# Gated scan and two feed-forward layers in one kernel: weight conversions of item 0 two steps sooner, the second chunk's tokens turned on TensorE

## The chip, the cores and the metric

The kernel runs on one core of a Trainium2 chip. The metric is the time of one execution on the device in microseconds (us), from the first instruction to the last result in memory; the median of several runs is quoted. A core has five engines that run their own instruction streams in order and wait for each other on semaphores: TensorE (PE in the profile, with its weight loads as PEld), VectorE (DVE), ScalarE (ACT), GpSimd (POOL) and SyncE (SP), which here issues most of the DMAs.

## The reference

Three stages follow one another over 2 x 6080 tokens of width 256:

```python
sig = 1.0 / (1.0 + np.exp(-f_logit))
f = lower_bound + (1.0 - lower_bound) * sig
h = f[:, t] * h + (1 - f[:, t]) * x[:, t]      # for each t in turn; y[:, t] = h
h1 = y @ w_in1;  z = (h1 - np.tanh(h1)) @ w_out1      # 256 -> 2048 -> 256
h2 = z @ w_in2;  out = np.maximum(0.01 * h2, h2) @ w_out2
```

Tokens, gates and output are fp32. The four weight matrices arrive as 64-bit floats and have to be turned into pairs of short fp32 numbers (a high and a low part) on the chip.

## The kernel before

**Chunks and items.** The 12160 tokens are cut into chunks of 1024. An *item* is one chunk in one of the two feed-forward layers; items 0 and 1 are chunks 0 and 1 in layer 0, item 2 is chunk 0 in layer 1, and from then on layer 0 of the next chunk and layer 1 of the one before alternate. Each item has 8 *units* (256 columns of the hidden width). Every product is done with high and low parts, as three fp32r matmuls.

**Steps of the first three items.** Items 0, 1 and 2 are plain products, written as four *steps* a unit, 32 steps an item, numbered s = 0 to 95. A step computes one 128 x 512 block of the hidden layer. In program order, step s issues: `plain(s)`, twelve LDWEIGHTS and MATMULs shown as six pairs or "x2" rows (line L441), into a PSUM bank from the list `hb`; on ScalarE the tanh `act(s)` (L451); on VectorE `shrink(s)` (L459, h - tanh h), which is the last reader of the bank; then for the step before, `hi(s-1)` on ScalarE (L464) and `lo(s-1)` on VectorE (L469); then the side jobs of that step, `work(s)`; and last, for the step three back, `emit_B(s-3)` (L485), which multiplies its hidden block by the unit's output weights `wb` into the banks `acc`. So TensorE sees plain(s), B(s-3), plain(s+1), B(s-2) and so on, and B(s-3) needs lo(s-3) and the unit's `wb`.

**Side jobs.** `put(p, jobs, q)` spreads a list of jobs evenly over the steps p to q - 1. During item 0 there are two sorts. *Conversions*: `first[u + 1]` turns the raw words of the input weights of unit u + 1 (`wa`) and the output weights of unit u (`wb`) into high and low parts. It has a load of 1 MB and eight jobs: s0 (ScalarE, L116), s1 (VectorE, L120 and L121), s2 (L127), s3 (L132, and two casts on ScalarE, L135), s4 (L138), s5 (L143) and twice s6 (L149), which write the low parts of `wa` and of `wb` and issue their copies to DRAM. In item 0 `wb` of unit u is read for the first time by B(4u), issued in step 4u + 3. *The front of chunk 1*: tokens of f_logit and x are loaded in pieces of 32 x 32 x 32 elements (`load_tokens`), turned on VectorE (L338), passed through tanh (L345), an affine gate with the columns `ga` and `gb` (VectorE, L349), a product (L356), and the scan (L367); then they are split into high and low parts (L396, L400).

**Start.** Chunk 0 is loaded in rows of 256 elements by `first_front` in two halves of 512 tokens; TensorE turns 128 x 128 blocks against an identity (L296) into PSUM banks that are not yet in use, and tanh, gate, product and scan (L302, L306, L310, L320) follow. Four loads are issued from ScalarE's DMA queue, three from SyncE's, all at the beginning.

Of the kernel before, what the change touches and what calls it, by code (L numbers as in the profile page):

```python
# [15 lines left out]
P = 128  # L16
# [4 lines left out]
def tile_gated_scan_two_ffn(  # L21
# [77 lines left out]
    def convert(parts):  # L99

        s = {}
        n = 2 * len(parts)
        sh = [P, 4, 2 * P]

        def words(i, dt):
            return s["raw"].bitcast(dt).rearrange("p a (n t) -> p a n t", t=2)[:, :n, :, i]

        def f0():
            s["raw"] = cv.tile(sh, U64, tag="raw", bufs=2, name="raw")
            for i, (src, _, _) in enumerate(parts):  # L110
                nc.sync.dma_start(s["raw"][:, 2 * i:2 * i + 2], src)

        def s0():
            s["t"] = cv.tile(sh, F32, tag="c", bufs=2, name="b")
            s["b"] = s["t"][:, :n]
            nc.scalar.activation(s["b"], words(1, F32), AF.Abs)  # L116

        def s1():
            b = s["b"].bitcast(I32)
            nc.vector.tensor_scalar(s["b"], s["b"], W_LO, W_HI, op0=ALU.max, op1=ALU.min)  # L120
            nc.vector.tensor_scalar(  # L121
                b, b, 3, 0x3FFFF000, op0=ALU.logical_shift_left, op1=ALU.bitwise_and
            )
# [12 lines left out]

        def s4():
            nc.vector.scalar_tensor_tensor(  # L138
                words(0, F32), words(0, U32), 2.0**-32, words(1, I32), op0=ALU.mult, op1=ALU.add
            )  # L140

        def s5():
            nc.vector.tensor_scalar(  # L143
                words(1, I32), s["b"].bitcast(I32), -(1 << 23), None, op0=ALU.bitwise_and
            )

        def s6(i):
            l, e = (words(j, F32)[:, 2 * i:2 * i + 2] for j in range(2))
            nc.vector.scalar_tensor_tensor(  # L149
                s["w"][i][1], l, 2.0**-20, e, op0=ALU.mult, op1=ALU.mult  # L150
            )
            parts[i][2]()

        return f0, [s0, s1, s2, s3, s4, s5] + [lambda i=i: s6(i) for i in range(len(parts))]
# [123 lines left out]
                src[t0:t0 + n, d0:d0 + 32].rearrange("(i c) r -> c i r", c=32),  # L278
            )

    def first_front(half, banks):

        t0, a = macros[0][0], half * H
        nb = H // P
        s = {}

# [3 lines left out]
                s[nm], {"f": ff, "x": xf}[nm][t0 + a:t0 + a + H].rearrange("(j p) d -> p j d", p=P)  # L290
            )

        def turn(nm):
            for k in range(KD):
                for j in range(nb):
                    nc.tensor.transpose(  # L296
                        banks[nm][k][:, j * P:(j + 1) * P], s[nm][:, j, k * P:(k + 1) * P], ident
                    )

        def s1(k):  # L300
            s["g", k] = fp.tile([P, H], F32, tag="f", bufs=2, name="g")
# [1 line left out]

        def s2(k):
            g = s["g", k]
            nc.vector.tensor_scalar(g, g, ga[:, k:k + 1], gb[:, k:k + 1], op0=ALU.mult, op1=ALU.add)  # L306

        def s4(k):
            s["v", k] = fp.tile([P, H], F32, tag="x", bufs=2, name="v")
# [2 lines left out]
            )  # L312

        def s5(k):
            if 0 not in ys:
                ys[0] = fp.tile([P, KD, 2 * H], F32, tag="y", name="y")
            y = ys[0][:, k]
            for p in range(0, H, H // 2):
                m = p + H // 2
                nc.vector.tensor_tensor_scan(  # L320
                    y[:, a + p:a + m], s["g", k][:, p:m], s["v", k][:, p:m],
                    y[:, a + p - 1:a + p] if a + p else 0.0, op0=ALU.mult, op1=ALU.subtract,
                )
            if half:
                nc.vector.tensor_copy(carry[:, k:k + 1], y[:, 2 * H - 1:2 * H])

        return load, turn, [lambda f=f, k=k: f(k) for f in (s1, s2, s4, s5) for k in range(KD)]

    def front(c, k):

# [214 lines left out]
    with tc.manual_schedule():  # L545
# [46 lines left out]
        put(4 * I + 16, [lambda: conv.__exit__(None, None, None)])  # L592


        for it in range(len(items) - 1):
            base = I * it
            l, c = items[it + 1]
            jobs = []
            if l == 0:
                at = ((8, 14) if it == 0 else (base - 4, base + 2))  # L600
# [3 lines left out]
            lead = 10 if it == 0 else 0 if l == 0 else 2 * NS  # L604
# [150 lines left out]
```

## Time and profile before

| | |
|---|---|
| median of 3 runs | 2047.53 us (2045.61 to 2047.65) |
| profiled execution | 2048.42 us, its span (first to last instruction) 2046.6 us |
| TensorE busy in the span | 1990.6 us, 97% |
| VectorE, ScalarE busy | 1429.3 us (70%), 1199.8 us (59%) |
| mean granted TensorE clock | 0.987 of full speed |
| chain that ended last | 91% TensorE, 5% VectorE |

The profiled execution is 0.9 us above the median, and 1.8 us of it lie outside the span. Shares of busy time over the whole span hide where TensorE waits; the stretches of the span have to be read one by one. A granted clock of 1.00 is 2.4 GHz, and the lower of the two levels is 1.2 GHz.

### The profile page before, as it was taken

To read this page: it belongs to the slowest core of one execution; us is meant where nothing else is said; L and a number is where in the kernel's file an instruction comes from. 1 tells how busy PE (TensorE), PEld (TensorE's weight loads), DVE (VectorE), ACT (ScalarE), POOL (GpSimd) and SP (SyncE) were. 2 spreads that over 40 slices of the span, in tenths; PEclk is the share of its full clock that TensorE was granted. 3 is DMA by queue.
4 is the path that set the end of the run, shared out by engine and by line. 5 is a ranking of instruction groups with operands and counts; after the bars stand their busy time and mean duration, and the time that the engine had idled before them with its cause. 6 is when DMAs were issued, how large, how long until landed. Compare 5 with 4: busy or idle time off the path is not lost.

```text
span 2046.6 us, 24457 instructions
## 1 busy us (share of the span) xinstructions
PE 1990.6 (97%) x8744; PEld 1652.0 (81%) x8744; DVE 1429.3 (70%) x2269; ACT 1199.8 (59%) x2185; POOL 0.7 (0%) x6
## 2 busy tenths in 40 slices
PE   5879999999999999999999999999999999999998
PEld 4668888888888888888888888888888888889887
DVE  6788887986776776776677677577677677666443
ACT  3445655665666566566566556566656656656554
POOL 0000000000000000000000000000000000000000
PEclk8989999999999999999999999999999999999999
DMA  4536777784563563563554555456356356354352
GB/s 158 150 134 216 233 240 257 267 260 133 173 180 142 162 183 142 162 183 141 163 170 155 162 162 162 142 169 175 142 162 183 141 162 178 142 162 170 141 162 86
DMA packets 384458, 348.30 MB, mean 170 GB/s; under 512 B 289104, under 2 KB 291152, under 8 KB 384336
## 3 DMA queue, kind: packets, MB, share of 16 engines
q1 hardware_dynamic: 382480, 345.17, 52.5%
q10 hardware_dynamic: 1856, 1.57, 0.2%
q8 instruction: 69, 1.13, 0.2%
q14 instruction: 53, 0.43, 0.1%
HBM read 309.07 MB, written 37.62 MB: 169 GB/s over the span
## 4 chain that ended last, share of the span: by engine, by line
PE 91%; DVE 5%; DMA 1%; ACT 1%; issue 1%; SPq 1%; DVEq 0%; ACTq 0%
PE acc L485 48%; PE b L428 22%; PE c L428 16%; PE b L441 3%; PE c L441 2%; DVE gl L469 1%; DVE g L459 1%; DVE raw L138 0%; SPq L508 0%; DMA out_dram<-o 0%; ACT b L116 0%; DMA wb<-st 0%; DVE b L127 0%; DMA wb<-wb 0%; ACT gh L464 0%
## 5 line engine op out<-in xcount | busy, mean ns | idle before, releaser
L485 PE MATMUL acc<-gh,wb 128*128 128x512 f32 (+1 forms) x3072 | 1043.9, 389 | 26.4 <-DVE wb L149 24.5
L485 PEld LDWEIGHTS acc<-gh,wb 128*128 128x128 f32 x3072 | 579.2, 189 | 146.0 <-DVE wb L149 27.3
L469 DVE TENSOR_TENSOR gl<-g,gh 128x512 fp32r<-128x512 f32 (+1 forms) x768 | 500.5, 679 | 222.5 <-ACT gh L464 214.3
L485 PE MATMUL acc<-gl,wb 128*128 128x512 f32 (+1 forms) x1536 | 597.2, 389 | 1.8 <-DVE gl L469 1.8
L464 ACT CAST gh<-g 128x512 fp32r<-128x512 f32 (+1 forms) x768 | 444.8, 615 | 86.7 <-DVE g L459 86.6
L428 PE MATMUL b<-xh,wa 128*128 128x512 f32 (+1 forms) x1344 | 492.6, 387 | 0.0
L428 PE MATMUL c<-xh,wa 128*128 128x512 f32 (+1 forms) x1008 | 362.6, 387 | 0.0
L485 PEld LDWEIGHTS acc<-gl,wb 128*128 128x128 f32 x1536 | 289.8, 189 | 61.2 <-DVE gl L469 3.8
L453 ACT ACTIVATE g<-c 128x512 f32<-128x512 f32 (+1 forms) x280 | 159.6, 602 | 247.2 <-PE c L428 226.1
L428 PEld LDWEIGHTS b<-xh,wa 128*128 128x128 f32 x1344 | 252.3, 188 | 49.2
L451 ACT ACTIVATE g<-c 128x512 f32<-128x512 f32 (+1 forms) x272 | 155.4, 602 | 209.8 <-PE c L428 168.2
L428 PE MATMUL b<-xl,wa 128*128 128x512 f32 (+1 forms) x672 | 260.0, 387 | 0.0
L428 PEld LDWEIGHTS c<-xh,wa 128*128 128x128 f32 x1008 | 189.2, 188 | 37.0
L459 DVE TENSOR_TENSOR g<-c,g 128x512 f32<-128x512 f32 (+1 forms) x272 | 177.7, 678 | 38.2 <-ACT g L451 35.3
L715 DVE TENSOR_TENSOR c<-b,s 128x512 f32<-128x512 f32 (+1 forms) x168 | 115.1, 685 | 116.2 <-PE b L428 114.5
L428 PE MATMUL c<-xl,wa 128*128 128x512 f32 (+1 forms) x504 | 195.0, 387 | 0.0
L661 ACT COPY c<-b 128x512 f32<-128x512 f32 (+1 forms) x168 | 94.9, 565 | 131.0 <-PE b L428 131.0
L695 DVE TENSOR_TENSOR c<-b,s 128x512 f32<-128x512 f32 (+1 forms) x168 | 116.1, 691 | 56.3 <-PE b L428 32.9
L459 DVE TENSOR_TENSOR g<-b,g 128x512 f32<-128x512 f32 (+1 forms) x112 | 76.4, 682 | 111.7 <-ACT g L451 111.5
L428 PEld LDWEIGHTS b<-xl,wa 128*128 128x128 f32 x672 | 126.1, 188 | 24.9
L684 ACT COPY s<-c 128x512 f32<-128x512 f32 (+1 forms) x168 | 98.1, 584 | 37.7 <-PE c L428 30.2
L428 PEld LDWEIGHTS c<-xl,wa 128*128 128x128 f32 x504 | 94.6, 188 | 18.6
(76 smaller groups left out, 1182.5 us busy)
## 6 DMA issues: line engine op xcount, KB each, us to landing
wa<-wa SPq DMA_DIRECT2D x168, 896.0 KB, 5.0
wb<-wb SPq DMA_DIRECT2D x192, 512.0 KB, 5.6
wa<-wa SPq DMA_DIRECT2D x24, 512.0 KB, 5.5
wa<-st SPq DMA_DIRECT2D x24, 512.0 KB, 3.4
out_dram<-o SPq DMA_DIRECT2D x176, 64.0 KB, 1.9
rawf<-in_f_logit_dram SPq DMA_DIRECT2D x80, 128.0 KB, 5.7
rawx<-in_x_dram SPq DMA_DIRECT2D x80, 128.0 KB, 3.0
raw<-in_moe_w_in_dram SPq DMA_DIRECT2D x16, 512.0 KB, 6.0
```

Of the source, the lines that this page charges most:

```text
L428: nc.tensor.matmul(bank[:, :h], wt[:, s, w], xx[:, v, :h], start=start and i == 0, stop=i == 2, skip_group_check=True,)
L441: nc.tensor.matmul(bank[:, :h], wt[:, s, 2 * k + j], xx[:, v[k], :h], start=i == 0, stop=i == 5,)
L451: nc.scalar.activation(g[:, :h], src[:, :h], AF.Tanh)
L453: nc.scalar.activation(g[:, :h], src[:, :h], AF.Prelu, alpha=0.01)
L459: nc.vector.tensor_tensor(g[:, :h], u["src", name][:, :h], g[:, :h], ALU.subtract)
L464: nc.scalar.copy(gh[:, :h], u["g", name][:, :h])
L469: nc.vector.tensor_tensor(gl[:, :h], u["g", name][:, :h], u["hi", name][:, :h].bitcast(F32), ALU.subtract)
L485: nc.tensor.matmul(bank[e][:, :h], w[:, j, s, es], v[:, :h], start=first and i == 0, stop=i == 2, skip_group_check=True,)
L661: nc.scalar.copy(c11[:, :h], b1[:, :h])
L684: nc.scalar.copy(s5[:, :h], c12[:, :h])
L695: nc.vector.tensor_tensor(c12[:, :h], b1[:, :h], s5[:, :h], ALU.add)
L715: nc.vector.tensor_tensor(c22[:, :h], b1[:, :h], s5[:, :h], ALU.add)
```

## The change

Five things change in the program. (1) In item 0 the conversion that writes `wa` of unit u + 1 and `wb` of unit u (u from 2) is put into steps 4u - 2 to 4u instead of 4u to 4u + 2, and its load at step 4u - 7 instead of 4u - 5; that of u = 1 into steps 2 to 4 instead of 3 to 5. (2) Chunk 1 is no longer loaded in small pieces and turned on VectorE: `first_front` gets the chunk as an argument, loads rows of 256 elements from SyncE's queue, and TensorE turns them, four 128 x 128 blocks at a time, into the bank `c12`, each of eight groups as a side job of a step between 9 and 28. `c12` leaves the list `hb`, which has three banks instead of four for all of items 0, 1 and 2. (3) The affine gate of both chunks becomes an ACTIVATE with Identity on ScalarE, with `ga` and `gb` as columns. (4) The first loads are reordered: SyncE issues the first raw weights and then x; ScalarE issues f_logit, `lower_bound`, and, behind its first three activations, the second raw weights and the second half of chunk 0. (5) Item 1 begins like item 0 with the order `order0`: four steps on the first half of the chunk over two units, then four on the second half.

```diff
-        def f0():
+        def f0(eng=nc.sync):
...
-                nc.sync.dma_start(s["raw"][:, 2 * i:2 * i + 2], src)
+                eng.dma_start(s["raw"][:, 2 * i:2 * i + 2], src)
...
-    def first_front(half, banks):
+    def first_front(c, half, banks):
...
-        t0, a = macros[0][0], half * H
+        t0, a = macros[c][0], half * H
...
-        def turn(nm):
-            for k in range(KD):
-                for j in range(nb):
...
+        def turn(nm, k):
+            for j in range(nb):
+                nc.tensor.transpose(
+                    banks[nm][k][:, j * P:(j + 1) * P], s[nm][:, j, k * P:(k + 1) * P], ident
+                )
...
-            nc.vector.tensor_scalar(g, g, ga[:, k:k + 1], gb[:, k:k + 1], op0=ALU.mult, op1=ALU.add)
+            nc.scalar.activation(g, g, AF.Identity, scale=ga[:, k:k + 1], bias=gb[:, k:k + 1])
...
-        load0("f", nc.sync)
-        load0("x", nc.scalar)
-        first[0][0]()
-        load1("f", nc.scalar)
-        first[1][0]()
-        load1("x", nc.scalar)
...
+        first[0][0]()
+        load0("f", nc.scalar)
+        load0("x", nc.sync)
         nc.scalar.dma_start(lb, lower_bound.rearrange("(k p) -> p k", p=P))
...
-        run(front0[0:2] + first[0][1][0:2] + front0[2:4] + first[0][1][2:4] + front0[4:8])
-        run(mix(split0[0:4], first[0][1][4:]))
+        run(first[0][1][0:1])
+        for nm in "fx":
+            turn0(nm, 0), turn0(nm, 1)
+        for k in range(KD):
+            front0[k][0]()
+        first[1][0](nc.scalar)
+        for nm in "fx":
+            load1(nm, nc.scalar)
+            turn1(nm, 0), turn1(nm, 1)
+        for k in range(KD):
+            front0[k][1]()
+        run(first[0][1][1:5])
+        run([front0[k][i] for i in (2, 3) for k in range(KD)])
+        run(mix(split0[0:4], first[0][1][5:]))
...
-        put(1, front1 + split0[4:8], 4)
-        put(3, first[2][1], 6)
+        put(1, mix(*front1) + split0[4:8], 4)
+        put(2, first[2][1], 5)
         for u in range(2, NU):
-            put(NS * u - 5, [first[u + 1][0]])
-            put(NS * u, first[u + 1][1], NS * u + 3)
-
+            put(NS * u - 7, [first[u + 1][0]])
+            put(NS * u - 2, first[u + 1][1], NS * u + 1)
+
+        split1 = make_forms(1)
         I = NS * NU
+        for half, a in ((0, 9), (1, 21)):
+            load, turn, stages = first_front(1, half, {nm: [c12, c12] for nm in "fx"})
+            put(a - 4, [lambda load=load, nm=nm: load(nm, nc.sync) for nm in "fx"], a - 3)
+            jobs = []
+            for k in range(KD):
+                f = stages[k]
+                jobs += [
+                    lambda turn=turn, k=k: turn("f", k), f[0], lambda f=f: (f[1](), None),
+                    lambda turn=turn, k=k: turn("x", k), f[2], f[3],
+                ]
+            put(a, jobs + split1[4 * half:4 * half + 4], a + 15 - half)
+
...
-        for it in range(len(items) - 1):
+        for it in range(1, len(items) - 1):
...
-        hb = b1s + [c11, c12]
+        hb = b1s + [c11]
...
-            order = order0 if it == 0 else []
+            order = order0 if it < 2 else []
...
-                u, name, bank = us[v], f"c{2 - j}{n + 1}", hb[s % 4]
+                u, name, bank = us[v], f"c{2 - j}{n + 1}", hb[s % 3]
```

Line numbers shift: L459, L469, L400, L485, L441 and L296 become L464, L474, L405, L490, L446 and L298 in the changed kernel. A number at the end of a name tells buffers apart.

VectorE, conversion of `wb` for unit 3 (B(12), the first to read it, is issued in step 15). Before, from `shrink(13)` on; `shrink(14)` writes g_578 and `wb` of unit 3 is wb_558:

```order
L459 TENSOR_TENSOR g_549<-b11_87,g_549 128x512
L469 TENSOR_TENSOR gl_554<-g_524,gh_552 128x512
L132 TENSOR_SCALAR raw_398<-raw_398 128x1024
L138 SCALAR_TENSOR_TENSOR raw_398<-raw_398 128x1024
L143 TENSOR_SCALAR raw_398<-b_531 128x1024
L349 TENSOR_SCALAR tf_486<-tf_486,ga_83,gb_84 128x512
L338 STREAM_TRANSPOSE tx_564<-rawx_430 128x512
L459 TENSOR_TENSOR g_578<-c11_88,g_578 128x512
L469 TENSOR_TENSOR gl_583<-g_549,gh_581 128x512
L149 SCALAR_TENSOR_TENSOR wa_557<-raw_398 128x512
L149 SCALAR_TENSOR_TENSOR wb_558<-raw_398 128x2x256
L338 STREAM_TRANSPOSE tx_599<-rawx_430 128x512
```

Now, from `shrink(11)` on; `shrink(12)` writes g_535, and the same `wb` is wb_514:

```order
L464 TENSOR_TENSOR g_505<-c11_88,g_505 128x512
L474 TENSOR_TENSOR gl_510<-g_480,gh_508 128x512
L132 TENSOR_SCALAR raw_360<-raw_360 128x1024
L138 SCALAR_TENSOR_TENSOR raw_360<-raw_360 128x1024
L143 TENSOR_SCALAR raw_360<-b_487 128x1024
L464 TENSOR_TENSOR g_535<-b10_86,g_535 128x512
L474 TENSOR_TENSOR gl_540<-g_505,gh_538 128x512
L149 SCALAR_TENSOR_TENSOR wa_513<-raw_360 128x512
L149 SCALAR_TENSOR_TENSOR wb_514<-raw_360 128x2x256
L312 SCALAR_TENSOR_TENSOR v_546<-g_466,c12_89 128x512
L464 TENSOR_TENSOR g_560<-b11_87,g_560 128x512
L474 TENSOR_TENSOR gl_565<-g_535,gh_563 128x512
```

The last instruction on `wb` stood behind `shrink(14)` and now stands behind `shrink(12)`; the turns (L338) and gates (L349) of chunk 1 are gone from VectorE, and the product L312 reads the bank c12.

VectorE, steps 3 to 5, the conversion of `wb` of unit 1. Before, from `lo(2)` on, with `shrink(4)` and `shrink(5)` writing g_323 and g_349 and `wb` of unit 1 being wb_332:

```order
L120 TENSOR_SCALAR b_303<-b_303 128x1024
L121 TENSOR_SCALAR b_303<-b_303 128x1024
L127 SCALAR_TENSOR_TENSOR b_303<-raw_235,b_303 128x1024
L459 TENSOR_TENSOR g_323<-b10_86,g_323 128x512
L469 TENSOR_TENSOR gl_328<-g_292,gh_326 128x512
L132 TENSOR_SCALAR raw_235<-raw_235 128x1024
L138 SCALAR_TENSOR_TENSOR raw_235<-raw_235 128x1024
L143 TENSOR_SCALAR raw_235<-b_303 128x1024
L459 TENSOR_TENSOR g_349<-b11_87,g_349 128x512
L469 TENSOR_TENSOR gl_354<-g_323,gh_352 128x512
L149 SCALAR_TENSOR_TENSOR wa_331<-raw_235 128x512
L149 SCALAR_TENSOR_TENSOR wb_332<-raw_235 128x2x256
```

Now, from the first instructions of that conversion on, with `shrink(3)`, `shrink(4)` and `shrink(5)` writing g_300, g_330 and g_353 and the same `wb` being wb_313:

```order
L127 SCALAR_TENSOR_TENSOR b_289<-raw_235,b_289 128x1024
L464 TENSOR_TENSOR g_300<-b10_86,g_300 128x512
L474 TENSOR_TENSOR gl_305<-g_272,gh_303 128x512
L405 TENSOR_TENSOR xl_208<-y_202,xh_207 128x512 x2
L132 TENSOR_SCALAR raw_235<-raw_235 128x1024
L138 SCALAR_TENSOR_TENSOR raw_235<-raw_235 128x1024
L143 TENSOR_SCALAR raw_235<-b_289 128x1024
L464 TENSOR_TENSOR g_330<-b11_87,g_330 128x512
L474 TENSOR_TENSOR gl_335<-g_300,gh_333 128x512
L149 SCALAR_TENSOR_TENSOR wa_312<-raw_235 128x512
L149 SCALAR_TENSOR_TENSOR wb_313<-raw_235 128x2x256
L464 TENSOR_TENSOR g_353<-c11_88,g_353 128x512
```

The first three conversion instructions now stand ahead of `shrink(3)`, and `wb` is written ahead of `shrink(5)` and `lo(4)` instead of behind them.

TensorE, around step 11. Before, the end of B(7), plain(11) into c12, and B(8):

```order
L485 MATMUL acc11_93<-gh_416,wb_332 128x512
L485 MATMUL acc11_93<-gl_418,wb_332 128x512
L485 MATMUL acc11_93<-gh_416,wb_332 128x512
L441 MATMUL c12_89<-xh_206,wa_331 128x512 x2
L441 MATMUL c12_89<-xl_207,wa_331 128x512 x2
L441 MATMUL c12_89<-xh_206,wa_331 128x512 x2
L485 MATMUL acc00_90<-gh_450,wb_456 128x512
L485 MATMUL acc00_90<-gl_452,wb_456 128x512
L485 MATMUL acc00_90<-gh_450,wb_456 128x512
```

Now, the end of B(7), plain(11) into c11, a turn, and B(8):

```order
L490 MATMUL acc11_93<-gh_432,wb_313 128x512
L490 MATMUL acc11_93<-gl_434,wb_313 128x512
L490 MATMUL acc11_93<-gh_432,wb_313 128x512
L446 MATMUL c11_88<-xh_207,wa_312 128x512 x2
L446 MATMUL c11_88<-xl_208,wa_312 128x512 x2
L446 MATMUL c11_88<-xh_207,wa_312 128x512 x2
L298 MATMUL c12_89<-ident_81,rawx_365 128x128 x4
L490 MATMUL acc00_90<-gh_455,wb_412 128x512
L490 MATMUL acc00_90<-gl_457,wb_412 128x512
L490 MATMUL acc00_90<-gh_455,wb_412 128x512
```

A group of four turns of x stands between plain(11) and B(8); it waits for its load and for the tanh that read the bank before. Seven more such groups stand in other steps from 9 to 28.

## Rows read from the trace of the kernel before

**Rows 1.** The page, part 2: tenths of TensorE busy, 40 slices of 51 us.
```profile
PE   5879999999999999999999999999999999999998
```

**Rows 2.** Busy time by stretch, us: PE, PEld, DVE, ACT, POOL, then granted clock, DMA.
```profile
53.36:155.99 102.63, 80.62 (x305) 63.46 (x304) 84.49 (x129) 44.83 (x76) 0.00 (x0) 0.88 0.46 136
...
155.99:242.90 86.91, 86.85 (x383) 71.54 (x382) 72.20 (x107) 49.17 (x87) 0.00 (x0) 1.00 0.67 217
```

**Rows 3.** Waits from 53.36 to 155.99 us: total us, times, longest.
```profile
PE acc L485 <- DVE wb L149: 21.2, 6, 5.1
DVE g L459 <- ACT g L451: 20.4, 8, 4.6
```

**Rows 4.** Timeline of unit 3: start us, us, engine, line, operation [idle before <-releaser].
```profile
85.71 0.69 DVE L149 SCALAR_TENSOR_TENSOR wb<-raw 128x512 fp32r<-128x512 f32 x1
...
86.45 0.73 PE L485 MATMUL acc<-gh,wb 128*128 128x512 f32 x2 [4.06 <-DVE wb L149]
...
87.65 1.05 PE L441 MATMUL b<-xh,wa 128*128 128x512 f32 x2
...
88.50 1.05 PE L441 MATMUL b<-xl,wa 128*128 128x512 f32 x2
```

**Rows 5.** Timeline of VectorE in unit 3, steps 13 and 14.
```profile
79.07 0.68 DVE L459 TENSOR_TENSOR g<-b,g 128x512 f32<-128x512 f32 x1
...
79.67 0.68 DVE L469 TENSOR_TENSOR gl<-g,gh 128x512 fp32r<-128x512 f32 x1
...
80.27 0.69 DVE L132 TENSOR_SCALAR raw<-raw 128x1024 int32<-128x1024 int32 x1
...
82.86 0.54 DVE L349 TENSOR_SCALAR tf<-tf,ga,gb 128x512 f32<-128x512 f32 x1
83.32 0.70 DVE L338 STREAM_TRANSPOSE tx<-rawx 128x512 f32<-128x512 f32 x1
83.94 0.65 DVE L459 TENSOR_TENSOR g<-c,g 128x512 f32<-128x512 f32 x1
```

**Rows 6.** VectorE groups by form, 53.36 to 155.99 us.
```profile
L338 DVE STREAM_TRANSPOSE tf<-rawf 128x512 f32<-128x512 f32 x4 | 2.7, 696 | 0.0
```

**Rows 7.** Timeline of the start.
```profile
2.39 0.92 ACTq L289 DMA_DIRECT2D rawx<-in_x_dram  x1
...
5.70 1.94 PE L296 MATMUL b<-ident,rawf 128*128 128x128 f32 x8 [5.70 <-DMA rawf<-in_f_logit_dram]
...
7.67 0.60 ACT L302 ACTIVATE g<-b 128x512 f32<-128x512 f32 x1 [0.26 <-PE b L296]
...
11.63 1.28 DVE L310 SCALAR_TENSOR_TENSOR v<-g,c 128x512 f32<-128x512 f32 x2
...
17.83 0.68 DVE L400 TENSOR_TENSOR xl<-y,xh 128x512 fp32r<-128x512 f32 x1
...
19.90 0.60 ACT L451 ACTIVATE g<-b 128x512 f32<-128x512 f32 x1 [3.58 <-PE b L441]
```

**Rows 8.** Line L296, the token turns: duration ns min/median/max.
```profile
L296 PE MATMUL b<-ident,rawf x8: 421/421/447, 5.7 to 7.2; 128*128 128x128 f32 x8
```

**Rows 9.** DMA issues of the first 20 us: KB each, median us to landing.
```profile
rawf<-in_f_logit_dram ACTq DMA_DIRECT2D x1, 512.0 KB, 10.3
```

**Rows 10.** Timeline of steps 2 to 6.
```profile
48.03 0.68 DVE L149 SCALAR_TENSOR_TENSOR wb<-raw 128x512 fp32r<-128x512 f32 x1
...
48.77 0.73 PE L485 MATMUL acc<-gh,wb 128*128 128x512 f32 x2 [3.30 <-DVE wb L149]
```

**Rows 11.** Timeline of VectorE at step 6.
```profile
53.36 0.69 DVE L459 TENSOR_TENSOR g<-c,g 128x512 f32<-128x512 f32 x1 [4.64 <-ACT g L451]
```

**Rows 12.** Timeline at the end of item 0.
```profile
154.94 0.74 PE L485 MATMUL acc<-gh,wb 128*128 128x512 f32 x2 [0.70 <-DVE wb L149]
...
155.99 0.40 PE L441 MATMUL b<-xh,wa 128*128 128x512 f32 x1
```

**Rows 13.** DMA issues from 120 to 160 us.
```profile
wa<-wa SPq DMA_DIRECT2D x5, 512.0 KB, 5.4
```

More of the change, by code (lines that the diff above doesn't have):

```diff
@@ L291, in load @@
             )
-        def turn(nm):
-            for k in range(KD):
-                for j in range(nb):
-                    nc.tensor.transpose(
-                        banks[nm][k][:, j * P:(j + 1) * P], s[nm][:, j, k * P:(k + 1) * P], ident
-                    )
+        def turn(nm, k):
[3 more added lines that the diff above has]
+                )
         def s1(k):
@@ L314, in s5 @@
         def s5(k):
-            if 0 not in ys:
-                ys[0] = fp.tile([P, KD, 2 * H], F32, tag="y", name="y")
-            y = ys[0][:, k]
+            if c not in ys:
+                ys[c] = fp.tile([P, KD, 2 * H], F32, tag="y", name="y")
+            y = ys[c][:, k]
             for p in range(0, H, H // 2):
                 m = p + H // 2
+                init = 0.0 if t0 + a + p == 0 else carry[:, k:k + 1] if a + p == 0 else (
+                    y[:, a + p - 1:a + p]
+                )
                 nc.vector.tensor_tensor_scan(
-                    y[:, a + p:a + m], s["g", k][:, p:m], s["v", k][:, p:m],
-                    y[:, a + p - 1:a + p] if a + p else 0.0, op0=ALU.mult, op1=ALU.subtract,
+                    y[:, a + p:a + m], s["g", k][:, p:m], s["v", k][:, p:m], init,
+                    op0=ALU.mult, op1=ALU.subtract,
                 )
@@ L325, in s5 @@
                 nc.vector.tensor_copy(carry[:, k:k + 1], y[:, 2 * H - 1:2 * H])
-        return load, turn, [lambda f=f, k=k: f(k) for f in (s1, s2, s4, s5) for k in range(KD)]
+        return load, turn, [[lambda f=f, k=k: f(k) for f in (s1, s2, s4, s5)] for k in range(KD)]
     def front(c, k):
@@ L553, in tile_gated_scan_two_ffn @@
         make_identity(nc, ident)
-        nc.scalar.dma_start(lb, lower_bound.rearrange("(k p) -> p k", p=P))
-        load0, turn0, front0 = first_front(0, {"f": b1s, "x": [c11, c12]})
-        load1, turn1, front1 = first_front(1, {"f": acc[0], "x": acc[1]})
-        load0("f", nc.sync)
-        load0("x", nc.scalar)
-        first[0][0]()
-        load1("f", nc.scalar)
-        first[1][0]()
-        load1("x", nc.scalar)
+        load0, turn0, front0 = first_front(0, 0, {"f": b1s, "x": [c11, c12]})
+        load1, turn1, front1 = first_front(0, 1, {"f": acc[0], "x": acc[1]})
+        first[0][0]()
+        load0("f", nc.scalar)
+        load0("x", nc.sync)
+        nc.scalar.dma_start(lb, lower_bound.rearrange("(k p) -> p k", p=P))
         nc.vector.tensor_scalar(ga, lb, -0.5, 0.5, op0=ALU.mult, op1=ALU.add)
         nc.vector.tensor_scalar(gb, lb, 0.5, 0.5, op0=ALU.mult, op1=ALU.add)
-        turn0("f"), turn0("x"), turn1("f"), turn1("x")
         split0 = make_forms(0)
-        run(front0[0:2] + first[0][1][0:2] + front0[2:4] + first[0][1][2:4] + front0[4:8])
-        run(mix(split0[0:4], first[0][1][4:]))
+        run(first[0][1][0:1])
[12 more added lines that the diff above has]
+        run(mix(split0[0:4], first[0][1][5:]))
         order0 = [(u, j, n) for n in range(2) for u in range(2) for j in range(2)]
@@ L599, in tile_gated_scan_two_ffn @@
             if l == 0:
-                at = ((8, 14) if it == 0 else (base - 4, base + 2))
+                at = (base - 4, base + 2)
                 for k in range(KD):
@@ L603, in tile_gated_scan_two_ffn @@
                     jobs += [f for stage in front(c, k) for f in stage]
-            lead = 10 if it == 0 else 0 if l == 0 else 2 * NS
+            lead = 0 if l == 0 else 2 * NS
             put(base + lead, jobs + make_forms(it + 1), base + I - 2)
```

## The prediction

> **What bounds the kernel now.** The page's slices come first: TensorE is full in nearly all 40, and the loss lies in the first three, some 150 us [rows 1]. So I read the table of stretches, which splits item 0 from what follows. From 155.99 us, where item 1 begins, to 242.90 us TensorE works 86.85 of 86.91 us at a granted clock of 1.00; these are its 32 steps, so one step (plain and B) costs 2.716 us of TensorE at 2.4 GHz. From step 6 of item 0 (53.36 us) to 155.99 us it is busy only 80.62 of 102.63 us, at a mean clock of 0.88, and VectorE 84.49 [rows 2]. The 26 steps there would take 26 x 2.716 = 70.6 us at full clock, so 32 us are lost: about 22 idle, 10 to the clock.
>
> The table of waits says for what: B waits for the low part of `wb` (L149) six times, 21.2 us, once a unit, and VectorE then waits 20.4 us for ScalarE's tanh, since the next plain stands behind that B [rows 3]. The timeline of unit 3 shows one round: `wb` starts at 85.71, B resumes at 86.45 after 4.06 us, and the next plain runs at half clock: two pairs of matmuls start 0.85 us apart, 0.425 each against 2.716/12 = 0.226 [rows 4]. Neither engine is full there; a dependency that comes round once a unit makes each wait for the other in turn.
>
> **The change part by part.**
>
> *Conversions two steps sooner.* The order of VectorE shows `wb` of unit 3 behind `shrink(12)` instead of `shrink(14)`. B(12) needs lo(12), which stands behind `shrink(13)`, so lo now comes last and `wb` is no longer what B waits for. No work is added; what is late next is whichever engine has more to do. Two floors give that.
>
> VectorE's floor, step 6 to step 31: the 84.49 us busy [rows 2], less what leaves. Eight turns go (four of f_logit [rows 6], as many of x); one occupies 83.32 to 83.94, 0.62 us, and one of the four gates there 82.86 to 83.32, 0.46 [rows 5]: 8 x 0.62 + 4 x 0.46 = 6.8. Two of chunk 1's splits move behind step 31, for the price of their like, a lo: 0.60 [rows 5], together 1.2. Left: 76.5 us, 2.94 a step.
>
> TensorE's floor: 70.6 us and the new turns. Eight took 1.94 us at the start, 0.243 each [rows 7]; chunk 1 has 32, so 7.8. Sum 78.4 us, 3.02 a step. The two floors are nearly equal, and TensorE now has the higher one.
>
> The Trainium skill speaks against this trade: "VectorE: DVE Perf Modes", section "The three transpose paths", gives 390 ns on TensorE against 311 on VectorE for a 128 x 128 bf16 tile. By the page 32 turns would be 12.5 us, an estimate, and the sum below 4.7 us longer. The rows have fp32, 0.243 in a train on TensorE and 0.62 for four blocks on VectorE; the sum goes by them.
>
> *Order of steps 3 to 5.* Between `shrink(2)` and `wb` of unit 1, which starts at 48.03 [rows 10], VectorE now has the same instructions as before less `shrink(5)` and lo(4), 0.60 each [rows 5]: `wb` comes 1.2 us sooner. Behind it B(2), which began its wait of 3.30 us with the clock falling [rows 10], and plain(6) ran at half clock, and `shrink(6)` came 53.36 - 48.03 = 5.3 us after `wb` [rows 10, 11]. Now plain(4), and with it plain(5), waits longer for the splits, so TensorE arrives later and waits for `wb` under 1 us; if its clock is up, four matmuls of B(2) and twelve of plain(6) at 0.226 instead of 0.425 save up to 3; I take 1.4, since part of B ran fast already. The bounds are 0 and 3.
>
> *Start.* ScalarE now issues four loads (0.92 us the dearest, [rows 7]) behind its two tanh, then gates; before, the second tanh began at 7.67. With fewer loads beside that of f_logit I put the tanh's end at 7.5, the issues at 10.0, the gates (0.60 each, as a tanh [rows 7]) at 10.6 and 11.2. VectorE's first product began at 11.63 and the last split 6.2 us later [rows 7], with one conversion piece more between them than now; so the split starts at 16.8 at the latest instead of 17.83, and the first act at 18.9 against 19.90 [rows 7]: 1.0 us gained. The second half's x must land and be turned before plain(0): eight turns, 1.94, end by 16.8 if it lands within 5 us of its issue. Issued from this queue with everything in flight, a load took 10.3 us [rows 9]; then x lands at 20.3, is turned by 22.2, and plain(0) ends 3 us later than now. The bounds are +1 and -3; I take +1, because half as much is in flight. The Trainium skill, "ScalarE: Activation LUTs", section "What ACT_TABLE_LOAD costs", adds about 93 ns for each column operand of an ACTIVATE. Two columns would make the gate 0.79 us, an estimate, and the start 0.2 later.
>
> *Three banks.* Plain(s) needs `shrink(s-3)`. B(s-4), just ahead of it on TensorE, needs lo(s-4), which is the very next instruction on VectorE after `shrink(s-3)`. So I cost the missing bank at nothing; the cover is that B. If that cover were gone it would be a rival (below).
>
> *`order0` in item 1, and loads.* The weights of its second unit are needed at step 34 instead of 36, 5.4 us sooner; their load takes 5.4 [rows 13] and is issued on SyncE's queue behind the last copy of `wb`, in step 28. I count 0 and allow 2. Chunk 1's loads come four steps ahead of their turns.
>
> *Sum.* `shrink(6)` moves from 53.36 to 53.36 - 1.0 - 1.2 - 1.4 = 49.8. Plain(6), which began at about 49.6 (48.77 and 0.8 for four matmuls), starts 2.2 sooner, at 47.4. TensorE's floor ends at 47.4 + 78.4 = 125.8, VectorE's at 49.8 + 76.5 = 126.3, while the first plain of item 1 needs only lo(28) and B(28), some 3 us earlier. Floors are not reached: conversions are lumpy, VectorE's load is 98% of TensorE's, and each stops the other now and then. For that I add 2.5 us, a choice (0.1 a step). Item 1 starts at 128.3 instead of 155.99: 27.7 us gained. Behind it nothing is faster or slower, as TensorE is full there [rows 2]. The profiled execution took 2048.4, so 2020.7; the median of the runs lies 0.9 lower: **2020 us**.
>
> **The rivals.**
>
> 1. *The clock stays down.* With short waits every step, TensorE may run part of each unit at 1.2 GHz. A dozen slow matmuls more cost 12 x 0.2 = 2.4 us; in five units 12 us: 2032. For it: rows 4. Against it: after a wait of 0.70 us [rows 12] the matmuls were back at 0.40 us of duration each, as fast ones have.
> 2. *Turns cost more amid products.* Alone a turn lasts 0.421 us [rows 8]; if none overlap, 32 take 13.5 instead of 7.8, and as TensorE has the higher floor it all shows: 2026. This is also the side on which the skill's page on VectorE lies.
> 3. *The wait for `wb` is replaced by one for raw words or turns.* A conversion whose raw words land late, or a turn that stands ahead of B with its load missing, stops TensorE once a unit as now. Six waits as now put back 21.2 of the 27.7 us [rows 3]: 2041. Against it: loads are issued some five steps ahead.
> 4. *Slower: three banks in items 1 and 2.* Those 64 steps have TensorE full now, so each delay shows. From the end of plain(s-3) to plain(s) TensorE has five halves of a step, 6.8 us, while tanh and shrink take 1.3. If VectorE's queue held the shrink back over 6.8 us on average, the kernel would lose; from 0.43 us a step on (28/64) it would end slower than before: 2052 at 0.5.
>
> **How the numbers follow.** Forecast 0.77, rival 1 0.09, rival 2 0.06, rival 3 0.04, rival 4 0.02, and 0.02 for a gain that the start or another stall eats up. The forecast alone spans 2015 (nothing added, the clock's full 3 us) to 2028 (start 4 us worse, no gain at steps 3 to 5, wait in item 1). For 8 in 10, with rivals 1 and 2 in part, I give 2014 to 2031. A difference under 0.2% (4 us) can't be told from none in this kernel; faster by more: 0.95, same 0.02, slower 0.03.
>
> **What would show it.** Right: item 1 begins near 128 us; waits of B for L149 nearly vanish and are replaced by short ones for lo; VectorE is over 90% busy from step 6 to 28; the granted clock from about 50 us on is above 0.95; turns keep 0.243 in a train; ScalarE has one table load. Wrong: a clock near 0.88 again (rival 1), turns of 0.4 us each (rival 2), waits for a DMA ahead of turns or of L116 (rival 3), waits of plain for shrink in items 1 and 2 (rival 4), or plain(0) later than 20 us.

## The result, and the profile after

The changed kernel took 2022.24 us in the median of 4 runs (2021.03 to 2022.78), the kernel before 2047.11 beside it (2045.61 to 2047.65): the ratio is 0.9879, with a 95% interval of 0.9862 to 0.9896, so some 25 us are gone. Forecast was 2020, with 2014 to 2031. The profiled execution took 2021.03 us and its span is 2019.3 us; before, 2048.42 and 2046.6.

The page's line of TensorE and of its granted clock (40 slices of 50 us) answer to [rows 1]: of the three thin slices the first is left.

```profile
PE   4999999999999999999999999999999999999997
...
PEclk7999999999999999999999999999999999999999
```

The table of stretches of the changed kernel (us of PE, PEld, DVE, ACT, POOL, then granted clock, DMA share, GB/s). The second row runs from `shrink(6)` to the first plain of item 1 and answers to the first of [rows 2]: 78.37 us instead of 102.63. Two things are to be seen. VectorE was busy 75.20 us there, and the sum in the prediction was 76.5; and in the third row, from 55 to 125 us, it was busy 68.58 of 70 us, 98%, while TensorE was busy 93%, at a clock of 1.00. VectorE is now the fuller engine; e1, e5 and e8 below test whether it sets the pace.

```profile
16.00:18.00 2.00, 2.00 (x11) 2.00 (x11) 1.82 (x4) 0.35 (x1) 0.00 (x0) 0.50 0.04 13
53.19:131.56 78.37, 73.17 (x335) 59.52 (x334) 75.20 (x114) 46.05 (x79) 0.00 (x0) 1.00 0.54 183
55.00:125.00 70.00, 64.80 (x299) 52.59 (x298) 68.58 (x103) 41.27 (x71) 0.00 (x0) 1.00 0.49 169
```

The waits of the same stretch, which answer to [rows 3]. There is no row left for L149. What TensorE waits for are the turns L298: for the product that reads c12, for their tokens and for the tanh. VectorE waits for ScalarE's tanh 3.0 us instead of 20.4.

```profile
PE c L298 <- DVE v L312: 3.2, 2, 2.4
DVE g L464 <- ACT g L456: 3.0, 3, 1.4
...
PE c L298 <- DMA rawf<-in_f_logit_dram: 1.5, 1, 1.5
...
PE c L298 <- ACT g L304: 0.6, 1, 0.6
```

The timeline of the start answers to [rows 7]. The second tanh begins at 8.62, while the forecast had its end at 7.5, and the load of the second half's x is issued behind it, at 10.07. Its turns start at 17.26, and plain(0) waits for them until 18.83, though the last split (17.14) was early enough. The first act comes at 21.45 instead of 19.90.

```profile
6.64 1.94 PE L298 MATMUL b<-ident,rawf 128*128 128x128 f32 x8 [6.64 <-DMA rawf<-in_f_logit_dram]
...
8.62 0.60 ACT L304 ACTIVATE g<-b 128x512 f32<-128x512 f32 x1 [0.26 <-PE b L298]
...
10.07 0.53 ACTq L292 DMA_DIRECT2D rawx<-in_x_dram  x1
10.71 1.52 ACT L308 ACTIVATE g<-g,gb,ga 128x512 f32<-128x512 f32 x2 [1.49 <-DVE raw L138]
...
17.14 0.68 DVE L405 TENSOR_TENSOR xl<-y,xh 128x512 fp32r<-128x512 f32 x1
17.26 1.91 PE L298 MATMUL acc<-ident,rawx 128*128 128x128 f32 x8
...
18.83 1.20 PE L446 MATMUL b<-xh,wa 128*128 128x512 f32 x2
...
21.45 0.60 ACT L456 ACTIVATE g<-b 128x512 f32<-128x512 f32 x1 [5.10 <-PE b L446]
```

Steps 5 and 6 answer to [rows 10, 11]. `wb` of unit 1 starts at 48.36, later than before, and `shrink(6)` at 53.19, 4.8 us behind it instead of 5.3. With three banks in turn, the shrink that reads c11 at 50.46 is `shrink(5)`, which stood ahead of `wb` before; `shrink(6)` is the next one. TensorE begins plain(5) at 48.10 and plain(6) at 50.94.

```profile
48.10 0.70 PE L446 MATMUL c<-xh,wa 128*128 128x512 f32 x2
...
48.36 0.69 DVE L149 SCALAR_TENSOR_TENSOR wb<-raw 128x512 fp32r<-128x512 f32 x1
...
50.46 0.69 DVE L464 TENSOR_TENSOR g<-c,g 128x512 f32<-128x512 f32 x1 [1.41 <-ACT g L456]
...
50.94 0.62 PE L446 MATMUL b<-xh,wa 128*128 128x512 f32 x2
...
53.19 0.69 DVE L464 TENSOR_TENSOR g<-b,g 128x512 f32<-128x512 f32 x1 [1.44 <-ACT g L456]
```

The first turn of chunk 1, in step 9: four 128 x 128 blocks, and 0.36 us later the next product. In the other seven groups the next product starts 0.35 to 0.41 us behind the first block.

```profile
60.46 0.60 PE L298 MATMUL c<-ident,rawf 128*128 128x128 f32 x4
...
60.82 0.48 PE L490 MATMUL acc<-gh,wb 128*128 128x512 f32 x1
```

The end of item 0 answers to [rows 12]. The turn of f_logit behind plain(26) waits for the product that reads c12 (114.08), 2.42 us; the last low part of `wb` is written at 124.16; from 125.59 on VectorE waits for TensorE again; and item 1 starts at 131.56 instead of 155.99.

```profile
114.08 0.68 DVE L312 SCALAR_TENSOR_TENSOR v<-g,c 128x512 f32<-128x512 f32 x1
...
114.82 0.66 PE L298 MATMUL c<-ident,rawf 128*128 128x128 f32 x4 [2.42 <-DVE v L312]
...
124.16 0.69 DVE L149 SCALAR_TENSOR_TENSOR wb<-raw 128x512 fp32r<-128x512 f32 x1
...
125.59 0.69 DVE L464 TENSOR_TENSOR g<-c,g 128x512 f32<-128x512 f32 x1 [0.74 <-ACT g L456]
...
131.56 0.62 PE L446 MATMUL c<-xh,wa 128*128 128x512 f32 x2
```

### The profile page after: what moved, and what is told of

Its sections match the earlier page's. It is cut to its first block, busy times and chain, and to the rows that moved or that the text cites. A ratio compares the mean times of both kernels' runs of the same rounds, so it can differ in the third digit from the quotient of the medians.

```text
span 2019.3 us, 24484 instructions
## 1 busy us (share of the span) xinstructions
PE 1977.3 (98%) x8776; PEld 1647.6 (82%) x8776; DVE 1420.0 (70%) x2253; ACT 1205.1 (60%) x2193; POOL 0.7 (0%) x6
## 4 chain that ended last, share of the span: by engine, by line
PE 93%; DVE 4%; DMA 1%; SPq 1%; issue 1%; ACT 0%; ACTq 0%; DVEq 0%
PE acc L490 49%; PE b L433 22%; PE c L433 16%; PE b L446 3%; PE c L446 2%; DVE gl L474 1%; DMA rawf<-in_f_logit_dram 1%; DVE g L464 1%; SPq L276 0%; DMA out_dram<-o 0%; DVE raw L138 0%; SPq L513 0%; DVE y L325 0%; DVE b L121 0%; DVE o L509 0%
## 5 line engine op out<-in xcount | busy, mean ns | idle before, releaser
L490 PE MATMUL acc<-gh,wb 128*128 128x512 f32 (+1 forms) x3072 | 1039.2, 388 | 1.0 <-DVE o L509 1.0
L490 PEld LDWEIGHTS acc<-gh,wb 128*128 128x128 f32 x3072 | 577.4, 188 | 115.7 <-DVE o L509 2.0
L474 DVE TENSOR_TENSOR gl<-g,gh 128x512 fp32r<-128x512 f32 (+1 forms) x768 | 500.8, 680 | 221.0 <-ACT gh L469 212.7
L490 PE MATMUL acc<-gl,wb 128*128 128x512 f32 (+1 forms) x1536 | 595.3, 388 | 0.4 <-DVE gl L474 0.4
L469 ACT CAST gh<-g 128x512 fp32r<-128x512 f32 (+1 forms) x768 | 444.9, 615 | 85.4 <-DVE g L464 85.4
L490 PEld LDWEIGHTS acc<-gl,wb 128*128 128x128 f32 x1536 | 288.7, 188 | 57.8 <-DVE gl L474 1.2
L458 ACT ACTIVATE g<-c 128x512 f32<-128x512 f32 (+1 forms) x275 | 156.6, 603 | 248.0 <-PE c L433 226.9
L456 ACT ACTIVATE g<-c 128x512 f32<-128x512 f32 (+1 forms) x261 | 148.8, 601 | 193.9 <-PE c L433 161.7
L464 DVE TENSOR_TENSOR g<-c,g 128x512 f32<-128x512 f32 (+1 forms) x261 | 170.5, 679 | 32.7 <-ACT g L456 29.8
L464 DVE TENSOR_TENSOR g<-b,g 128x512 f32<-128x512 f32 (+1 forms) x123 | 83.9, 682 | 101.7 <-ACT g L456 101.6
```

The lines of the kernel that those rows point to most:

```text
L456: nc.scalar.activation(g[:, :h], src[:, :h], AF.Tanh)
L458: nc.scalar.activation(g[:, :h], src[:, :h], AF.Prelu, alpha=0.01)
L464: nc.vector.tensor_tensor(g[:, :h], u["src", name][:, :h], g[:, :h], ALU.subtract)
L469: nc.scalar.copy(gh[:, :h], u["g", name][:, :h])
L474: nc.vector.tensor_tensor(gl[:, :h], u["g", name][:, :h], u["hi", name][:, :h].bitcast(F32), ALU.subtract)
L490: nc.tensor.matmul(bank[e][:, :h], w[:, j, s, es], v[:, :h], start=first and i == 0, stop=i == 2, skip_group_check=True,)
```

## The experiments

Each kernel ran beside the kernel before on the same chip: the median of that one was 2047.99 us beside e1 to e4, 2047.63 beside e5 to e7, and 2048.52 beside e8 to e10. Where kernels of different groups are compared, it is "by the times" or "by the differences" to the kernel before (the changed kernel: 24.9 us).

**One part alone: the conversions (e1).** The kernel before, with

```diff
-        put(3, first[2][1], 6)
+        put(2, first[2][1], 5)
-            put(NS * u - 5, [first[u + 1][0]])
-            put(NS * u, first[u + 1][1], NS * u + 3)
+            put(NS * u - 7, [first[u + 1][0]])
+            put(NS * u - 2, first[u + 1][1], NS * u + 1)
```

> The kernel before with the conversions and their loads moved as in the change, and nothing else. Theory A (the wait for wb, once a unit, was the loss; without it VectorE's load sets the pace): VectorE has the eight turns and four gates still, 6.8 us more than in the changed kernel, and the start is that of before, 1.5 us better; so about 17 to 21 us faster than before, 2026 to 2030 us, with waits of B for L149 nearly gone and VectorE over 95% busy from step 8 on. Theory B (taking work off VectorE is what counts, the wait was only its symptom): less than 6 us faster, above 2041 us, with waits of B for L149 still there.

Measured: 2030.91 us, ratio 0.9918 (0.9905 to 0.9932), 17.1 us faster. The waits from 50 to 140 us (total, times, longest) show lo (L469) where `wb` stood, and VectorE is busy 67.04 of 70 us from 55 to 125:

```profile
PE acc L485 <- DVE gl L469: 11.9, 8, 2.8
```

```profile
55.00:125.00 70.00, 58.02 (x235) 44.64 (x234) 67.04 (x101) 32.96 (x57) 0.00 (x0) 0.96 0.55 150
```

Theory A holds. Moving the conversions removes the wait for `wb`; VectorE, with the turns and gates still on it, is then 96% busy, and TensorE waits for its lo.

**The other parts alone (e2).** The changed kernel, with the conversions back:

```diff
-        put(2, first[2][1], 5)
+        put(3, first[2][1], 6)
-            put(NS * u - 7, [first[u + 1][0]])
-            put(NS * u - 2, first[u + 1][1], NS * u + 1)
+            put(NS * u - 5, [first[u + 1][0]])
+            put(NS * u, first[u + 1][1], NS * u + 3)
```

> The changed kernel with the conversions and their loads back at the steps of before. Theory A: the wait for wb comes back once a unit; VectorE has 1 us less a unit to do ahead of wb, the start loses 1.5 us: 3 to 8 us faster than before, 2039 to 2044 us, six waits of B for L149 of 2.5 to 4 us and a granted clock below 0.92 in item 0. Theory B: most of the gain stays, below 2030 us.

Measured: 2037.18 us, ratio 0.9947 (0.9934 to 0.9961), 10.8 us faster. This is between the theories. The wait for `wb` is back six times, as A has it. Five of them, 13.3 us, lie between `shrink(6)`, here at 54.08, and item 1 at 146.67, where the kernel before has six and 21.2 [rows 3]; the clock there is 0.94, where A had it below 0.92 and the kernel before shows 0.88 [rows 2]:

```profile
PE acc L490 <- DVE wb L149: 13.3, 5, 4.0
```

```profile
54.08:146.67 92.59, 78.98 (x337) 62.46 (x336) 75.06 (x112) 46.23 (x79) 0.00 (x0) 0.94 0.44 152
```

VectorE was busy 9.4 us less than before in this stretch (75.06 against 84.49), and the stretch is 10.0 us shorter (92.59 against 102.63). What leaves VectorE comes back about one for one, where A had counted 1 us a unit. e1 and e2 together make 27.9 us, the whole change 24.9: part of what each gains is the same wait.

**Three banks (e3).** The kernel before, with

```diff
-        hb = b1s + [c11, c12]
+        hb = b1s + [c11]
-                u, name, bank = us[v], f"c{2 - j}{n + 1}", hb[s % 4]
+                u, name, bank = us[v], f"c{2 - j}{n + 1}", hb[s % 3]
```

> The kernel before with three banks in hb instead of four, nothing else. Theory A (lo, one VectorE instruction behind shrink, is waited for by the B that stands ahead of the plain, so the fourth bank has no use): within 2 us of before. Rival 4 of the prediction (plain waits for shrink in the 64 steps of items 1 and 2): 0.1 us a step or more, over 6 us slower than before.

Measured: 2047.38 us in 11 runs against 2047.99 in 15, ratio 0.9999 (0.999 to 1.0008). The fourth bank had no use in the kernel before; rival 4 falls.

**The old start (e4).** The changed kernel with the loads and first instructions in the order of before:

```diff
+        nc.scalar.dma_start(lb, lower_bound.rearrange("(k p) -> p k", p=P))
+        load0("f", nc.sync)
+        load0("x", nc.scalar)
+        first[0][0]()
+        load1("f", nc.scalar)
+        first[1][0]()
+        load1("x", nc.scalar)
...
+        f0 = [front0[k][i] for i in range(4) for k in range(KD)]
+        run(f0[0:2] + first[0][1][0:2] + f0[2:4] + first[0][1][2:4] + f0[4:8])
+        run(mix(split0[0:4], first[0][1][4:]))
```

> The changed kernel with the order of the first loads and of the first instructions on VectorE, ScalarE and TensorE as before (the gates stay on ScalarE). Theory A (the first act came 1.55 us later than before, since the second half's tokens were issued behind two tanh and landed late): 1 to 2 us faster than the changed kernel, first act at 19.9 us or sooner. Theory B (the start is taken up by slack in steps 0 to 6, which gained 4.4 us): within 0.5 us of the changed kernel.

Measured: 2020.95 us, ratio 0.9868 (0.9855 to 0.9882), 27.0 us faster than before and so 2.2 more than the changed kernel (1.3 by the two times themselves). The first act on ScalarE's timeline:

```profile
19.69 0.60 ACT L456 ACTIVATE g<-b 128x512 f32<-128x512 f32 x1 [3.27 <-PE b L446]
```

A holds: the new start costs most of what it loses at the first act (21.45 against 19.69); item 1 starts at 130.20, 1.4 us sooner than in the changed kernel. The 4.4 us in theory B come from taking `shrink(5)` of the changed kernel for `shrink(6)`; 1.7 is right.

**Gates back on VectorE (e5).** The changed kernel, with

```diff
-            nc.scalar.activation(g, g, AF.Identity, scale=ga[:, k:k + 1], bias=gb[:, k:k + 1])
+            nc.vector.tensor_scalar(g, g, ga[:, k:k + 1], gb[:, k:k + 1], op0=ALU.mult, op1=ALU.add)
```

> The changed kernel with the affine gates back on VectorE (eight of 0.46 us, four of them in steps 9 to 28). Theory A (VectorE sets the pace of steps 9 to 28): 1.5 to 3 us slower than the changed kernel, item 1 begins at 133 us or later. Theory B (TensorE has the higher floor, as the prediction put it): within 0.7 us of the changed kernel.

Measured: 2023.88 us, ratio 0.9882 (0.9867 to 0.9897): 1.6 us slower than the changed kernel by the times, 1.1 by the differences. In the profile item 1 starts 2.3 us later:

```profile
133.84 0.62 PE L446 MATMUL c<-xh,wa 128*128 128x512 f32 x2
```

The stretch from `shrink(6)` to `shrink(29)` tells more than the times. The changed kernel (first row) takes 72.40 us with VectorE busy 70.14; with the gates (second row) it is 74.31 with 72.04:

```profile
53.19:125.59 72.40, 67.20 (x309) 54.60 (x308) 70.14 (x105) 43.37 (x74) 0.00 (x0) 1.00 0.50 173
```

```profile
53.62:127.93 74.31, 68.63 (x309) 55.78 (x308) 72.04 (x110) 40.33 (x70) 0.00 (x0) 0.98 0.49 168
```

So 1.9 us of work on VectorE made the stretch 1.9 us longer, one for one, as A says. By the times alone it would not be told from B with certainty.

**Chunk 1's jobs ahead of the conversion's (e6).** The changed kernel with the loop that puts the conversions written behind the one that puts chunk 1's jobs; in a step that has both, the product L312 then comes before L149.

```diff
-        for u in range(2, NU):
-            put(NS * u - 7, [first[u + 1][0]])
-            put(NS * u - 2, first[u + 1][1], NS * u + 1)
-
         split1 = make_forms(1)
...
             put(a, jobs + split1[4 * half:4 * half + 4], a + 15 - half)
 
+        for u in range(2, NU):
+            put(NS * u - 7, [first[u + 1][0]])
+            put(NS * u - 2, first[u + 1][1], NS * u + 1)
```

> The changed kernel with the jobs of chunk 1 ahead of the conversion's jobs where both stand in one step. Theory A (a turn stands on TensorE ahead of a B that could run, and waits for the product L312, which stands behind two conversion instructions on VectorE; those waits of 2.42 and 0.75 us cost what they last at the end of item 0): 1 to 3 us faster than the changed kernel, waits of L298 for L312 below 1.5 us in all. Theory B (VectorE is the bound, TensorE only waits while it is ahead): within 0.7 us.

Measured: 2022.82 us, ratio 0.9877 (0.9862 to 0.9892), the same as the changed kernel. The waits of TensorE from 50 to 140 us, and two rows of its timeline:

```profile
PE c L298 <- DVE v L312: 2.4, 2, 2.2
PE acc L490 <- DVE gl L474: 1.9, 2, 1.5
```

```profile
116.55 1.05 PE L446 MATMUL b<-xh,wa 128*128 128x512 f32 x2
...
131.72 0.62 PE L446 MATMUL c<-xh,wa 128*128 128x512 f32 x2
```

The wait for L312 became shorter and one for lo (L474) took its place, with half-clock matmuls behind it; item 1 starts at 131.72. The time is as B has it. The waits for L312 did not fall below 1.5 us, as A asked, so what their going would give back is not shown; moving them in the queue only put another wait for VectorE in their place.

**Early loads at the start (e7).** The changed kernel, with the second half's tokens and the second raw weights issued at once, and from two queues:

```diff
         nc.scalar.dma_start(lb, lower_bound.rearrange("(k p) -> p k", p=P))
+        load1("f", nc.scalar)
+        first[1][0]()
+        load1("x", nc.scalar)
...
-        first[1][0](nc.scalar)
         for nm in "fx":
-            load1(nm, nc.scalar)
             turn1(nm, 0), turn1(nm, 1)
```

> The changed kernel with the second half's tokens issued from ScalarE's queue and the second raw weights from SyncE's, both right at the start instead of behind the two tanh; all else as changed. Theory A (late landing of the second half's x holds up plain(0)): first act below 20.3 us, 1 to 2.5 us faster than the changed kernel. Theory B (seven loads in flight delay f_logit and x of the first half as much as is won, or later slack takes it up): within 0.5 us.

Measured: 2018.96 us, ratio 0.9857 (0.9841 to 0.9873), 28.7 us faster than before. From its timeline: the second half is turned from 12.03 and 13.79 on instead of 15.50 and 17.26, and the first act comes at 18.52, 2.9 us sooner:

```profile
12.03 1.97 PE L298 MATMUL acc<-ident,rawf 128*128 128x128 f32 x8 [1.54 <-DMA rawf<-in_f_logit_dram]
...
13.79 1.91 PE L298 MATMUL acc<-ident,rawx 128*128 128x128 f32 x8
...
18.52 0.60 ACT L456 ACTIVATE g<-b 128x512 f32<-128x512 f32 x1 [2.73 <-PE b L446]
```

A holds, and more than the range it gave: the gain over the changed kernel is 3.3 us by the times, 3.8 by the differences.

**Conversions one step sooner still (e8), chunk 1's loads sooner (e9), both (e10).** On top of e7:

```diff
-            put(NS * u - 2, first[u + 1][1], NS * u + 1)
+            put(NS * u - 3, first[u + 1][1], NS * u)
```

for e8, and for e9

```diff
-            put(a - 4, [lambda load=load, nm=nm: load(nm, nc.sync) for nm in "fx"], a - 3)
+            put(a - 7, [lambda load=load, nm=nm: load(nm, nc.sync) for nm in "fx"], a - 6)
```

> The kernel of the run with early second-half loads, with the conversions of units 2 to 7 one step sooner still (steps 4u - 3 to 4u - 1). Theory A (VectorE sets the pace from step 8 on, and still idles some 3 us in steps 5 to 7, which conversion work could fill): 1 to 3 us faster than that kernel, 2016 to 2018 us, item 1 begins at 127 to 128 us. Theory B (TensorE's own work, or the start, is the bound by now): within 0.7 us of it, 2019 us.

> The kernel of the run with early second-half loads, with the loads of chunk 1 seven steps instead of four ahead of the turns. Theory A (VectorE is the bound; a turn that waits for its load only uses up TensorE's lead): within 0.7 us of that kernel, though the waits of L298 for a DMA are gone. Theory B (these waits, 1.5 to 2.3 us, come on top): 1 to 2.5 us faster.

> Both together. Theory A: as the run with the conversions sooner alone, within 0.7 us. Theory B: 1 us or more faster than either alone.

Measured: e8 2016.21 us, ratio 0.9845 (0.9831 to 0.9858); e9 2018.69, 0.9857 (0.9844 to 0.9871); e10 2016.76, 0.9845 (0.9831 to 0.9858). From 45 to 55 us VectorE was busy 6.92 us in e7 and 8.34 in e8 (first row e7, then e8), and in e8 item 1 starts at 125.38:

```profile
45.00:55.00 10.00, 10.00 (x45) 8.22 (x45) 6.92 (x11) 4.94 (x9) 0.00 (x0) 0.99 0.84 285
```

```profile
45.00:55.00 10.00, 10.00 (x45) 8.26 (x44) 8.34 (x12) 6.00 (x10) 0.00 (x0) 1.00 0.90 305
```

```profile
125.38 0.62 PE L446 MATMUL c<-xh,wa 128*128 128x512 f32 x2
```

In e9 no wait of L298 for a DMA is left from 20 to 140 us, and the one for L312 is 3.2 us instead of 1.5:

```profile
PE c L298 <- DVE v L312: 3.2, 2, 2.8
```

For e8 theory A holds: 2.5 us less than e9 on the same chip, and 2.7 less than e7 by the times; item 1 starts even sooner than A gave. For e9 alone the two can't be told apart: 0.3 us under e7 by the times, 1.2 by the differences. On top of e8 the sooner loads bring nothing (e10, 0.6 us over e8 on the same chip); but e8 has no wait of a turn for a DMA left from 50 to 140 us, so there was none for them to remove. e8 is the fastest of all, 32.3 us under the kernel before.

## Why the prediction was right, and where it was not

*The wait for `wb` and its removal.* Right. e1 alone brings 17 of the 25 us, and no L149 row is left among the waits.

*Two floors, TensorE's the higher.* The step that failed is the price of a turn, and with it which engine is the fuller. VectorE's floor was about met: 76.5 forecast, 75.2 up to item 1 and 76.1 to the end of lo(31). TensorE's was put at 78.4 with 0.243 us a turn, taken from the train at the start. The eight groups amid products took 3.0 us in all instead of 7.8, under 0.10 a turn, so TensorE's floor is 73.6, the lower one, and VectorE is the bound (e1, e5, e8).

The reason is the clock, not the place. The price was taken at the lower clock and added to products priced at 2.4 GHz. In e8 two trains of eight stand one behind the other at the start, with nothing else on TensorE between them:

```profile
11.62 1.09 PE L298 MATMUL acc<-ident,rawf 128*128 128x128 f32 x8 [1.32 <-DMA rawf<-in_f_logit_dram]
13.51 1.82 PE L298 MATMUL acc<-ident,rawx 128*128 128x128 f32 x8 [0.80 <-DMA rawx<-in_x_dram]
```

```profile
11.60:12.70 1.10, 1.08 (x8) 0.86 (x8) 1.06 (x3) 0.00 (x0) 0.00 (x0) 1.00 0.93 329
13.80:15.30 1.50, 1.50 (x9) 1.45 (x7) 1.47 (x4) 0.72 (x2) 0.00 (x0) 0.50 0.00 0
```

The first train ran at a granted clock of 1.00 and took 1.09 us, the second almost wholly at 0.50 and took 1.82. The duration of one turn (ns, min/median/max) tells the level. In the changed kernel the train at 17.26, at 0.50, has 421; the turns of f_logit amid products, at 1.00, have 273; and the train of the kernel before, whose 1.94 us were used, had 421 [rows 8]:

```profile
L298 PE MATMUL acc<-ident,rawx x8: 421/421/421, 17.3 to 18.8; 128*128 128x128 f32 x8
```

```profile
L298 PE MATMUL c<-ident,rawf x16: 271/273/331, 60.5 to 115.2; 128*128 128x128 f32 x16
```

For that train the views show a clock of 1.00, but the trace of the kernel before has no record of the clock ahead of 15.59 us, and its turns last as long as those at 0.50. Rival 2 (0.42 a turn) took the duration at the same lower clock for the price and is wrong by more. The Trainium skill's page "VectorE: DVE Perf Modes" ("The three transpose paths") gives TensorE 390 ns for a bf16 tile; no turn in this place comes near it, and the measurement decides.

*What was added for stops.* From plain(6) (50.94) to item 1 are 80.6 us, and the forecast had 80.9: 70.6 of products, 7.8 of turns and 2.5 of stops. Measured are 70.6, 3.0 and the rest, 7.0, of which the turns' waits make 5.3. Two terms are wrong by some 4.5 us each and cancel; that this stretch came out right is luck. I had let item 1 begin some 3 us ahead of VectorE's end, as if TensorE still had its lead of three steps then. VectorE at 98% uses that lead up: at 125.59 it is VectorE that waits, plain(29) has just ended, and TensorE's 2.5 steps to plain(32), 6.8 us at 2.716, all lie behind that.

*Start.* Wrong in sign: 1.0 us to be gained, 1.55 lost, inside its bound of 3. f_logit landed later than taken (its turn starts at 6.64), so the loads behind the second tanh were issued from 8.62 on, and plain(0) waited for x; e4 and e7 show it by undoing it in two ways. The gate on ScalarE took 0.81 us (two in 1.52), not 0.60. The sentence of the Trainium skill ("ScalarE: Activation LUTs", "What ACT_TABLE_LOAD costs") made it 0.79, an estimate; the trace agrees.

*Steps 3 to 6.* `wb` of unit 1 came 1.2 us sooner but for the start's loss, as forecast: 48.03 + 1.55 - 1.2 = 48.38, and 48.36 was measured. Mis-sized is the clock's term: 1.4 us were to be gained between `wb` and `shrink(6)`, and 0.5 came. B(2) does not wait any more, and plain(6) runs at 2.4 GHz; but plain(5) begins only at 48.10, and behind it and B(2) plain(6) can't begin before 50.94. The bound of 3 was too high as well, since it counts twelve matmuls of plain(6), which has six.

*The sum.* Item 1 starts 24.4 us sooner where 27.7 were forecast. Of the 3.3 us between them 2.55 are the start's and 0.9 the clock's term; the stretch behind `shrink(6)`, with its two errors, was right within 0.2. The two spans differ by 27.3, more than the start of item 1. The forecast had nothing faster behind it, and items 1 and 2 are faster (changed kernel, then before):

```profile
131.56:305.64 174.08, 174.08 (x769) 144.19 (x768) 144.50 (x218) 102.15 (x180) 0.00 (x0) 1.00 0.72 239
```

```profile
155.99:331.19 175.20, 174.75 (x769) 143.99 (x768) 142.69 (x215) 100.98 (x177) 0.00 (x0) 1.00 0.72 238
```

They take 174.1 to 174.6 us in the changed kernel and the eight made from it (e2, e4 to e10), and 175.2 to 175.3 in the kernel before and the two made from that (e1, e3). So 1.1 us of the gain lies there. It comes neither from the conversions (e1), the banks (e3), the start (e4) nor the gates (e5); whether from chunk 1's new front or from `order0`, no run here tells. The last 1.8 us lie in code that all kernels share, and I take them for scatter: it took 1713.6 in the changed kernel, 1715.4 before, and 1714.3 to 1717.3 in the other ten. The medians are 24.9 us apart; the start of item 1 and these 1.1 us make 25.5.

*The rivals.* The clock stayed up (1). The wait did not come back as another of its size (3): the turns' waits make 5.3 us. Moving jobs past them brought nothing (e6), and e9, without those for a DMA, brought 0.3 to 1.2. Three banks cost nothing (4, e3).

## What to carry to other kernels

A wait that comes round once a unit, in which two engines stand still in turn, is worth more than the work of either: put what it waits for where another dependency already comes later. Then add up each engine's load for the stage and look which is nearest to full; from there on only that engine's work counts (e5, e8), and a wait of the other may only change its place when jobs are reordered (e6). Take every price at the clock at which it will be paid: a turn that lasted 421 ns at the start was no measure for one of 273 ns later, and such durations tell the level where the clock's row has no record yet.

## What the runs showed of the hardware

Eight turns of a 128 x 128 fp32 block in one train at the start took 1.91 us at a granted clock of 0.50 (the changed kernel, 17.26), and 1.09 us (e8) and 1.04 us (e4) at 1.00; four amid products at 1.00 took 0.35 to 0.41 us. So it is the clock that makes the factor of two or more between the start and the dense stretch.

Turns alone were followed by a rise of the clock. In e4 TensorE had run nothing but three trains of turns, from 5.68, 10.25 and 12.33 us on, when within the third one the duration of a turn fell from 421 to 273 ns; the first record of the clock, 1.00, begins there, at 13.81 us. The fourth train ran at that level throughout:

```profile
L298 PE MATMUL acc<-ident,rawf x8: 273/421/475, 12.3 to 13.8; 128*128 128x128 f32 x8
```

```profile
L298 PE MATMUL acc<-ident,rawx x8: 272/272/273, 14.0 to 14.7; 128*128 128x128 f32 x8
```
